# A decode kernel's projection and GLU: products over 32 equal columns, and zero products between them

## The chip, the core and the metric

The kernel runs on one core of a Trainium2 chip. The metric is the device time of one execution in microseconds (us), the median of several runs. Five engines work side by side and meet only at semaphores: TensorE (PE in the profile, its weight loads PEld) for matrix products into PSUM, VectorE (DVE), ScalarE (ACT), GpSimd (POOL) and SyncE (SP), whose queue here issues nearly all loads. 16 DMA engines carry the bytes.

## The reference

One token (D = 640) goes through a decoder layer: pre-norm attention over a cache of 4096 positions with 32 heads of 128, an output projection with a residual, then a pre-norm gated GLU with 1728 hidden columns and a second residual. Cut to what matters:

```python
def _A_ref(x, k_cache, v_cache, wq, wo):          # 32 heads, Dh = 128, Sk = 4096
    q = (x @ wq) per head
    scores = einsum("bhqd,bhkd->bhqk", q, k_cache) * Dh ** -0.5
    o = einsum("bhqk,bhkd->bhqd", softmax(scores), v_cache)
    return o.reshape(B, Sq, Hq * Dh) @ wo
def _B_ref(x, w_gate, w_up, w_down):
    return (gelu(x @ w_gate) * (x @ w_up)) @ w_down
h = x + _A_ref(_layernorm(x), k_cache, v_cache, wq, wo)
h2 = h + _B_ref(_layernorm(h), w_gate, w_up, w_down)
```

All inputs are bf16. The caches are 33.5 MB each, wq and wo 5.2 MB each, w_gate, w_up and w_down 2.2 MB each.

## The kernel before

**Order of the work.** Every engine has a list of operations written out by hand (class Prog). An operation waits for the semaphores of those that it depends on; products on TensorE run in the order of its list. `warm(e, n)` issues n products of a zero tile none_b with 512 columns into a PSUM bank that nobody reads then; `held` issues a product without a weight load of its own, so that the weights of the product before it are used again. In the profile, products that `held` issues have its line, L167.

**Start.** SP issues wq and the first K tile; ScalarE's queue issues x. GpSimd fills constants. TensorE runs 22 no-ops (L321), then x_cols (L325) turns x into columns, and a LayerNorm gives xlnB (L342; VectorE waits at L341 for the memset of xlnB first). q_proj (L354) waits for xlnB and wq.

**Attention.** Four tiles of 8 heads go through a loop on TensorE (L429). For each, VectorE multiplies K by q (L405), TensorE folds the products (L371), VectorE adds up the rest (L417), ScalarE takes the exponentials (L418), VectorE spreads them out (L424), and TensorE multiplies with V (L389) and sums by head (L395). Zero products stand in the loop in three places. K and V loads wait on SP until the tile that they overwrite has been read.

**Tail, which the change touches.** After the loop TensorE's list goes:
- z_sum (L464), the sums of the exponentials; VectorE then divides (L467, L468) and spreads out (L469), a product (L471) sorts, and VectorE copies to aP (L473).
- A product with the identity puts x into ps_p (L496).
- proj(0) and proj(16) (L501): 5 groups of outputs by 16 rows of wo each, 80 weight loads of 128 x 128 with one column of aP each. The first half waits for aP and the first half of wo, the second for the second half of wo. VectorE copies the result to hT (L507).
- LayerNorm (L331 to L337, with a product of the means at L332), hX (L515), and products that put the residual into ps_d (resid, L511), then hlnT (L518).
- glu (L531) twice, gate and then up: 75 weight loads with one column of hlnT each; the first waits for hlnT and w_gate, the second for w_up. VectorE and ScalarE make the GELU (L537 to L544) beside the second, and L545 multiplies with it.
- down (L552): 15 rows of products, four side by side in the array, then last_weights (L562) loads weights ahead, and the last four products (L565) wait for the last piece of w_down. VectorE and ScalarE copy (L567, L568), and two DMAs write the output.

SP's order in the tail: wo in two halves, small pieces of w_down into wd_lo, then, once the last V tile has been used, w_gate, w_up and four pieces of w_down (L491 to L493).

Of the kernel before, what the change touches and what calls it, by code (L numbers as in the profile page):

```python
# [7 lines left out]
ALU = mybir.AluOpType  # L8
# [156 lines left out]
def held(e, out, lhsT, rhs, start, stop):  # L165

    built = e.matmul(out, lhsT, rhs, start=start, stop=stop)  # L167
    old = built.ins
    bb = e.bass.cur_bb.bb
    new = mybir.InstMatmult(  # L170
        start_tensor_calc=old.start_tensor_calc, stop_tensor_calc=old.stop_tensor_calc, tile_size=old.tile_size,
        tile_position=old.tile_position, ldweights=False, name=old.name, engine=old.engine, debug=old.debug,
        ins=old.ins, outs=old.outs, sync_info=old.sync_info)
    insts = bb.instructions
    assert insts[-1].name == old.name
    del insts[-1]
    insts.append(new)
    return bass.BassInstruction(new)


def bass_sequential_preLN__gqa_block_cached__glu_gated_geglu__decode_kernel(nc, A_x, A_k_cache, A_v_cache, A_wq, A_wo, B_x, B_w_gate, B_w_up, B_w_down, out):
# [15 lines left out]
    xx = sb("xx", [128, 10], FP32)  # L197
    ln = sb("ln", [128, 8], FP32)
    xlnB = sb("xlnB", [128, 5, 64], BF16)
    hT = sb("hT", [128, 10], FP32)  # L200
    hX = sb("hX", [128, 128, 5], FP32)
    hlnT = sb("hlnT", [128, 5], BF16)
# [4 lines left out]
    aP = sb("aP", [128, 32], BF16)  # L207
    of_i = sb("of_i", [128, 32], BF16)
    g_t = sb("g_t", [128, 15], FP32)
# [3 lines left out]
    gu = sb("gu", [128, 15], FP32)  # L213
    hm = sb("hm", [128, 15], BF16)
# [4 lines left out]
    none_b = sb("none_b", [128, 128], BF16)  # L219
    wd_lo = sb("wd_lo", [64, 2, D], BF16)  # L220
    own_g = sb("own_g", [128, 15], FP32)
    id_f = sb("id_f", [128, 128], FP32)
# [7 lines left out]
    ps_g, ps_u, ps_p = bank[0], bank[1], bank[2]  # L230
# [4 lines left out]
    ps_z = bank[7]  # L235

    wo_sb = k_all[:, 0:32 * D].rearrange("p (i n) -> p i n", i=32)
# [3 lines left out]
    P = Prog(nc)  # L241
    V = lambda fn, *d: P.op("vector", fn, *d)
    A = lambda fn, *d: P.op("scalar", fn, *d)
    T = lambda fn, *d: P.op("tensor", fn, *d)
# [21 lines left out]
    def load_v(j, *after):  # L266
# [6 lines left out]
    c_xz = GP(lambda e: e.memset(xlnB[:, :, :], 0.0))  # L273
# [8 lines left out]
    c_idf = GP(lambda e: e.affine_select(id_f[:, :], ones_f[:, :], pattern=[[1, 128]], compare_op=ALU.is_equal,  # L282
                                         fill=0.0, base=0, channel_multiplier=-1), c_ones)
# [10 lines left out]
    for t in range(4):  # L294
        at = slice(32 * t, 32 * t + 32)
# [4 lines left out]
    for t in range(4):  # L300
        at = slice(32 * t, 32 * t + 32)
        c_of = GP(lambda e, at=at: e.affine_select(of_i[at, :], ones_b[at, 0:32], pattern=[[-1, 32]], compare_op=ALU.is_equal,
                                                   fill=0.0, base=0, channel_multiplier=1), c_of)
    c_none = GP(lambda e: e.memset(none_b[:, :], 0.0), c_of)
    GP(lambda e: e.memset(own_g[:, 0:13], 1.0))
    c_gm = GP(lambda e: e.memset(own_g[:, 13:15], 0.0), c_none)
    for lo in (0, 32):
        c_gm = GP(lambda e, lo=lo: e.affine_select(own_g[lo:lo + 32, 13:15], ones_f[lo:lo + 32, 0:2], pattern=[[0, 2]],
                                                   compare_op=ALU.is_ge, fill=0.0, base=15, channel_multiplier=-1), c_gm)
# [3 lines left out]
    def idle(eng, n):  # L313

        def fn(e):
            for _ in range(n):
                i = e.nop(hint="n", nofuse=True)
            return i
        return P.op(eng, fn)

    idle("tensor", 22)  # L321

    def x_cols(e):
        for c in range(5):
# [3 lines left out]
    xc = V(lambda e: e.tensor_copy(xx[:, 0:5], ps_s[:, 0:5]), xt)  # L328

    def layernorm(src, ev, out_fn, between=lambda: None):  # L330
        s2 = V(lambda e: e.tensor_mul(src[:, 5:10], src[:, 0:5], src[:, 0:5]), ev)  # L331
        m = T(lambda e: e.matmul(ps_s[:, 16:26], mean_f[:, :], src[:, 0:10], start=True, stop=True), s2, c_mean)  # L332
        l1 = V(lambda e: e.reduce_sum(ln[:, 0:2], ps_s[:, 16:26].rearrange("p (a c) -> p a c", a=2), axis=AX.X), m)
        l2 = V(lambda e: e.scalar_tensor_tensor(out=ln[:, 2:3], in0=ln[:, 0:1], scalar=ln[:, 0:1],
                                                in1=ln[:, 1:2], op0=ALU.mult, op1=ALU.subtract), l1)
        l3 = A(lambda e: e.activation(ln[:, 3:4], ln[:, 2:3], ACTF.Ln, bias=eps_t[:, 0:1], scale=-1.0), l2, c_eps)
        l4 = A(lambda e: e.activation(ln[:, 4:5], ln[:, 3:4], ACTF.Exp, bias=zero_t[:, 0:1], scale=-0.5), l3)  # L337
        between()
        return V(out_fn, l4)

    xz = P.op("vector", None, c_xz)  # L341
    xl = layernorm(xx, xc, lambda e: e.tensor_scalar(  # L342
        xlnB[:, :, :].rearrange("p c (a b) -> p c a b", a=4)[:, :, 0:4:3, :],
        xx[:, 0:5].unsqueeze(2).unsqueeze(3).to_broadcast([128, 5, 2, 16]), ln[:, 0:1], ln[:, 4:5],
# [27 lines left out]
            r = mm(e, bank[2 * i + s], id_b[:, :], prod[:, i, 32 * s:32 * s + 32, 16 * n:16 * n + 16], start=(n == 0), stop=(n == 7))  # L372
        return r

    def warm(e, n, load=False):
        for k in range(n):
            mm = e.matmul if load and k == 0 else lambda *a, **kw: held(e, *a, **kw)
            r = mm(ps_z, none_b[:, :], none_b[:, :].unsqueeze(1).to_broadcast([128, 4, 128]), start=True, stop=True)  # L378
        return r

    def fold(e, i):
# [40 lines left out]
    def block(j, s):  # L422
# [5 lines left out]
    T(None, c_idb, c_hs, c_none)  # L428
    lp = P.loop("tensor", range(NG), [  # L429
        ("wa", lambda e, j: warm(e, 8, True), lambda j: [landed["K", j, 0]], False),  # L430
        ("f00", lambda e, j: fold(e, 0), lambda j: [mults[j, 0, 0], reds[j - 1, 1] if j else qa], True),
        ("f01", lambda e, j: fold(e, 1), lambda j: [mults[j, 0, 1]], True),
        ("wb", lambda e, j: warm(e, 12), lambda j: [], False),
        ("f10", lambda e, j: fold(e, 0), lambda j: [mults[j, 1, 0], reds[j, 0]], True),
        ("f11", lambda e, j: fold(e, 1), lambda j: [mults[j, 1, 1]], True),
# [9 lines left out]
    for j in range(NG):  # L445
# [10 lines left out]
        if j < NG - 1:  # L456
# [2 lines left out]

    rt = GP(lambda e: e.tensor_tensor(out=RT[:, :, :], in0=RS[:, :].unsqueeze(2).to_broadcast([128, 2 * NG, 8]),  # L460
                                     in1=own8[:, :].unsqueeze(1).to_broadcast([128, 2 * NG, 8]), op=ALU.mult), exps[NG - 1, 1])
    def z_sum(e):
        for s in range(2):
            i = e.matmul(ps_z[:, 0:H], ones_f[:, :], RT[:, s::2, :], start=(s == 0), stop=(s == 1))  # L464
        return i
    z = T(z_sum, rt, c_ones)
    zr = V(lambda e: e.reciprocal(zt[:, :], ps_z[:, 0:H]), z)  # L467
    at = V(lambda e: e.tensor_tensor(out=aT[:, :], in0=ps_a[:, 0:H], in1=zt[:, :], op=ALU.mult), zr, lp.ev[NG - 1, "h"])  # L468
    as_ = V(lambda e: e.tensor_tensor(out=aS[:, :, :], in0=aT[:, :].unsqueeze(2).to_broadcast([128, H, 4]),  # L469
                                      in1=own[:, :].unsqueeze(1).to_broadcast([128, H, 4]), op=ALU.mult), at)  # L470
    sp = T(lambda e: e.matmul(ps_z[:, 32:64], aS[:, :, :].rearrange("p h q -> p (h q)"), of_i[:, :],  # L471
                              start=True, stop=True), as_, c_of)
# [20 lines left out]
    d_wd = [down_load(0, 0, 4), down_load(1, 0, 5), down_load(2, 0, 3), down_load(2, 3, 4)]  # L493


    T(lambda e: e.matmul(ps_p[:, 0:5], id_f[:, :], xx[:, 0:5], start=True, stop=False, skip_group_check=True), xc, c_idf)  # L496
    def proj(lo):
        def fn(e):
            for c in range(5):
                for i in range(lo, lo + 16):  # L500
                    r = e.matmul(ps_p[:, c:c + 1], wo_sb[:, i, c::5], aP[:, i:i + 1], start=False, stop=(i == 31),  # L501
                                 skip_group_check=True)
            return r
        return fn
    T(proj(0), ap, d_wo[0])
    pr = T(proj(16), d_wo[1])
    h = V(lambda e: e.tensor_copy(hT[:, 0:5], ps_p[:, 0:5]), pr)  # L507
    col = (0, 320, 160, 480)
    def resid(e):
        for q in range(4):  # L510
# [3 lines left out]
    def residual():  # L514
        hx = V(lambda e: e.tensor_tensor(out=hX[:, :, :], in0=id_f[:, :].unsqueeze(2).to_broadcast([128, 128, 5]),  # L515
                                         in1=hT[:, 0:5].unsqueeze(1).to_broadcast([128, 128, 5]), op=ALU.mult), h)
        T(resid, hx)
    hl = layernorm(hT, h, lambda e: e.tensor_scalar(  # L518
        hlnT[:, :], hT[:, 0:5], ln[:, 0:1], ln[:, 4:5], ALU.subtract, ALU.mult), residual)


    def glu(ps, w, cs, *deps):
        def fn(e):
            for c in cs:
                for m in range(15):
                    if m < 13:
                        lo, k = at_row[m]
                        ws = w[:, c, lo:lo + 127 * k + 1:k]
                    else:
                        ws = w[:, c, 16 * m - 208:16 * m - 80]  # L530
                    i = e.matmul(ps[:, m:m + 1], ws, hlnT[:, c:c + 1],  # L531
                                 start=(c == 0 and m == 0), stop=(c == 4), skip_group_check=True)
            return i
        return T(fn, *deps)
    ga = glu(ps_g, wg_sb, range(5), hl, d_wg)
    up = glu(ps_u, wu_sb, range(5), d_wu)
    g1 = V(lambda e: e.tensor_tensor(out=g_t[:, :], in0=ps_g[:, 0:15], in1=own_g[:, :], op=ALU.mult), ga, c_gm)  # L537
    g2 = V(lambda e: e.tensor_mul(t1[:, :], g_t[:, :], g_t[:, :]), g1)
    g3 = V(lambda e: e.scalar_tensor_tensor(out=t2[:, :], in0=t1[:, :], scalar=1.0 / GELU_C1, in1=g_t[:, :],
                                            op0=ALU.add, op1=ALU.mult), g2)  # L540
# [1 line left out]
    g7 = V(lambda e: e.tensor_scalar(t2[:, :], e_t[:, :], 1.0, None, ALU.add), g5)  # L542
    g8 = V(lambda e: e.reciprocal(t1[:, :], t2[:, :]), g7)
    g6 = V(lambda e: e.tensor_mul(gu[:, :], g_t[:, :], t1[:, :]), g8)  # L544
    g9 = V(lambda e: e.tensor_mul(hm[:, :], gu[:, :], ps_u[:, 0:15]), g6, up)  # L545

    def down(ms, qs=range(4)):
        def fn(e):
# [11 lines left out]
    def last_weights(e):  # L560
        for q in range(4):
# [4 lines left out]
                                start=False, stop=True), d_wd[3]) for q in range(4)]  # L566
# [35 lines left out]
```

The softmax here doesn't subtract the row's maximum and nothing guards it: scores larger than these inputs give would overflow.

## Time and profile before

| what | value |
| --- | --- |
| median of 7 runs | 201.99 us (201.87 to 202.56) |
| the profiled execution | 202.13 us |
| its span, first to last instruction | 200.9 us |
| PE, PEld, DVE busy | 137.8, 29.4, 103.7 us |
| bytes, mean rate | 84.31 MB, 420 GB/s |
| mean granted TensorE clock | 0.846 |

The page gives each engine's busy time; products overlap in the array, so PE's busy time is not the time in which columns stream through. The granted clock (PEclk) is given in parts of full speed. A line of the timeline has the start, the length, the engine, the line, the operation, the tiles, the count, and in brackets the idle time ahead and what ended it; a line can hold a group. The view by stage sums the engines' busy time over a stretch of the span. The chain that ended last follows back from the last instruction what released each.

### The profile page before, as it was taken

The numbers are of one execution on the slowest core, as the hardware profiler recorded it, in microseconds if no ns is written. First come the engines' busy times: TensorE is split into PE (matmuls) and PEld (weight loads), VectorE is DVE, ScalarE is ACT, GpSimd is POOL, SyncE is SP. The second block draws the span as 40 slices with busy tenths as digits, with TensorE's granted clock in tenths as the row PEclk, the third lists the DMA queues.
The fourth block names the chain that finished last, engine by engine and source line by source line (L and its number), as shares of the span: only waits on it lengthen the run. The fifth ranks groups of instructions, "written<-read, shape, count | busy, mean of one in ns | idle before, by whom it ended". The sixth has DMA issues, their size and how long they took to land.

```text
span 200.9 us, 2115 instructions
## 1 busy us (share of the span) xinstructions
PE 137.8 (69%) x1118; PEld 29.4 (15%) x742; DVE 103.7 (52%) x58; ACT 9.4 (5%) x27; POOL 7.3 (4%) x32
## 2 busy tenths in 40 slices
PE   0108001899887628898972589889789889778675
PEld 0103000000001300000031000000320000367574
DVE  0200001969945029998420596994996985120320
ACT  2100000000000100000000000000010000000100
POOL 6500000000000000000000000000000000200000
PEclk9999855569999957999998558999999999995555
DMA  9999999999999999999999999799999998999992
GB/s 327 449 478 418 418 418 418 418 418 470 509 447 431 418 431 418 418 418 431 418 418 418 418 522 496 320 405 418 437 509 418 418 431 385 424 432 416 427 402 114
DMA packets 2699, 84.31 MB, mean 420 GB/s; under 512 B 323, under 2 KB 518, under 8 KB 902
## 3 DMA queue, kind: packets, MB, share of 16 engines
q1 hardware_dynamic: 2690, 84.23, 97.8%
q8 instruction: 4, 0.07, 0.1%
q14 instruction: 1, 0.01, 0.0%
q10 hardware_dynamic: 4, 0.00, 0.0%
HBM read 84.23 MB, written 0.00 MB: 419 GB/s over the span
## 4 chain that ended last, share of the span: by engine, by line
DMA 51%; DVE 28%; PE 19%; ACT 1%; issue 1%; SPq 0%; DVEq 0%
DMA k_all<-in_A_k_cache_dram 42%; DVE prod L405 22%; PE psum L167 11%; DMA v_all<-in_B_w_up_dram 9%; PE psum L389 4%; DVE sc L417 3%; PE psum L531 1%; DVE p_bd L424 1%; PE psum L371 1%; PE psum L552 1%; DVE sc L414 1%; DVE sc L415 1%; PE psum L395 1%; ACT pt L418 0%; SPq L59 0%
## 5 line engine op out<-in xcount | busy, mean ns | idle before, releaser
L405 DVE TENSOR_TENSOR prod<-k_all,qb 128x8192 bf16<-128x8192 bf16 x16 | 70.3, 4420 | 41.1 <-DMA k_all<-in_A_k_cache_dram 35.5
L167 PE MATMUL psum<-prod,id_b 128*128 128x512 bf16 x240 | 58.7, 401 | 0.0
L167 PE MATMUL psum<-none_b 128*128 128x512 bf16 x132 | 35.0, 420 | 0.0
L378 PE MATMUL psum<-none_b 128*128 128x512 bf16 x4 | 2.2, 550 | 25.3 <-DMA k_all<-in_A_k_cache_dram 25.3
L389 PE MATMUL psum<-v_all,p_bd 128*32 128x512 bf16 x256 | 14.5, 380 | 4.7 <-DVE p_bd L424 4.7
L417 DVE TENSOR_REDUCE sc<-psum 128x128 f32<-128x2048 f32 x6 | 13.7, 2286 | 5.2 <-PE psum L167 5.2
L371 PEld LDWEIGHTS psum<-prod,id_b 128*128 128x128 bf16 x16 | 1.6, 97 | 77.5 <-issue 43.5
L371 PE MATMUL psum<-prod,id_b 128*128 128x512 bf16 x16 | 6.6, 414 | 8.6 <-DVE prod L405 5.8
L389 PEld LDWEIGHTS psum<-v_all,p_bd 128*32 128x32 bf16 x256 | 6.4, 97 | 37.1 <-DVE p_bd L424 30.9
L424 DVE TENSOR_TENSOR p_bd<-pt,own 128x1024 bf16<-128x1024 bf16 x8 | 9.8, 1222 | 2.2 <-ACT pt L418 2.2
L418 ACT ACTIVATE pt<-sc,zero_t 128x128 bf16<-128x128 f32 x8 | 3.2, 401 | 140.2 <-DVE sc L417 120.4
L354 PE MATMUL psum<-v_all,xlnB 128*32 128x512 bf16 x40 | 4.5, 630 | 6.9 <-DMA v_all<-in_A_wq_dram 6.9
L501 PE MATMUL psum<-aP,k_all 128*128 128x1 bf16 x160 | 6.7, 178 | 1.0 <-DMA k_all<-in_A_wo_dram 0.9
L460 POOL TENSOR_TENSOR RT<-RS,own 128x64 f32<-128x64 f32 x1 | 1.3, 1324 | 162.3 <-ACT pt L418 162.3
L501 PEld LDWEIGHTS psum<-aP,k_all 128*128 128x128 bf16 x160 | 6.6, 131 | 1.2 <-DMA k_all<-in_A_wo_dram 1.0
L395 PE MATMUL psum<-hs,po_sb 128*128 128x8 f32 x32 | 4.2, 258 | 3.2 <-ACT po_sb L458 3.2
L531 PE MATMUL psum<-hlnT,v_all 128*128 128x1 bf16 x150 | 5.5, 173 | 1.2 <-DMA v_all<-in_B_w_up_dram 1.2
L363 DVE CAST qb<-psum 128x512 bf16<-128x512 f32 x1 | 0.7, 692 | 9.9 <-PE psum L354 9.9
L531 PEld LDWEIGHTS psum<-hlnT,v_all 128*128 128x128 bf16 x150 | 5.3, 120 | 1.8 <-DMA v_all<-in_B_w_up_dram 1.3
L414 DVE TENSOR_REDUCE sc<-psum 128x64 f32<-128x1024 f32 x2 | 2.4, 1224 | 5.2 <-PE psum L167 5.2
L325 PE MATMUL psum<-one_bf,x_row 1*128 1x1 bf16 x5 | 0.4, 177 | 6.9 <-DMA x_row<-in_A_x_dram 6.9
L395 PEld LDWEIGHTS psum<-hs,po_sb 128*128 128x128 f32 x32 | 3.9, 191 | 5.1 <-issue 5.1
(75 smaller groups left out, 33.4 us busy)
## 6 DMA issues: line engine op xcount, KB each, us to landing
k_all<-in_A_k_cache_dram SPq DMA_DIRECT2D x2, 4096.0 KB, 19.1
v_all<-in_A_wq_dram SPq DMA_DIRECT2D x1, 5120.0 KB, 15.2
k_all<-in_A_wo_dram SPq DMA_DIRECT2D x2, 2560.0 KB, 29.2
v_all<-in_B_w_gate_dram SPq DMA_DIRECT2D x1, 2160.0 KB, 13.1
v_all<-in_B_w_up_dram SPq DMA_DIRECT2D x1, 2160.0 KB, 17.9
k_all<-in_B_w_down_dram SPq DMA_DIRECT2D x1, 800.0 KB, 20.5
k_all<-in_B_w_down_dram SPq DMA_DIRECT2D x1, 640.0 KB, 19.0
k_all<-in_B_w_down_dram SPq DMA_DIRECT2D x1, 480.0 KB, 21.1
```

The lines of the kernel that those rows point to most:

```text
L167: built = e.matmul(out, lhsT, rhs, start=start, stop=stop)
L354: i = e.matmul(ps_q[32 * t:32 * t + 32, :], xlnB[:, c, 32 * a:32 * a + 32], wq_j[:, c, t, a, :, :], start=(c == 0 and a == 0), stop=(c == ...
L371: mm = held if n or not first else lambda e, *a, **k: e.matmul(*a, **k)
L389: i = e.matmul(ps_o[a:a + 32, :], p_bd[:, s, 4 * b:4 * b + 4, :].rearrange("p g j -> p (g j)"), vt[:, 4 * b:4 * b + 4, :], start=(s == 0 a ...
L395: i = e.matmul(ps_a[:, bass.ds(at, 8)], po_sb[:, 128 * r:128 * r + 128], hs[:, r, :], start=(r == 0), stop=(r == 3))
L405: mults[j, s, i] = VM(lambda e: e.tensor_tensor(out=prod[:, i, :, :], in0=kt[:, 64 * c:64 * c + 64, :], in1=qb[:, j, :].unsqueeze(1).to_br ...
L414: V(lambda e: e.reduce_sum(sc[:, 64:128], g16(0, 1024), axis=AX.X), folds[j, s, 1], free)
L417: reds[j, s] = VR(lambda e: e.reduce_sum(sc[:, :], g16(0, 2048), axis=AX.X), folds[j, s, 1], free)
L418: exps[j, s] = AS(lambda e: e.activation(pt[:, :], sc[:, :], ACTF.Exp, bias=zero_t[:, 0:1], scale=INV_SQRT_DH, accum_out=RS[:, 2 * j + s:2 ...
L424: blocks[j, s] = VB(lambda e: e.tensor_tensor(out=p_bd[:, hf, :, :], in0=pt[:, :].unsqueeze(2).to_broadcast([128, 128, 8]), in1=own8[:, :] ...
L501: r = e.matmul(ps_p[:, c:c + 1], wo_sb[:, i, c::5], aP[:, i:i + 1], start=False, stop=(i == 31), skip_group_check=True)
L531: i = e.matmul(ps[:, m:m + 1], ws, hlnT[:, c:c + 1], start=(c == 0 and m == 0), stop=(c == 4), skip_group_check=True)
```

## The change

The 22 no-ops become one. VectorE's own wait for the memset goes; TensorE's x_cols waits for a later memset of the same engine, and VectorE waits for x_cols. The projection and both GLU products read their one column 32 times, and write 32 equal columns, of which one is read. Twenty-six zero products, with one weight load in each of five groups, are put into ps_u, the bank of the second GLU product: 3 ahead of z_sum, 4 behind it, 8 between the halves of the projection, 5 ahead of the residual products and 6 between the GLU halves.

```diff
-    idle("tensor", 22)
+    idle("tensor", 1)
...
-    xz = P.op("vector", None, c_xz)
...
-    def warm(e, n, load=False):
+    def warm(e, n, load=False, at=ps_z):
...
-            r = mm(ps_z, none_b[:, :], none_b[:, :].unsqueeze(1).to_broadcast([128, 4, 128]), start=True, stop=True)
+            r = mm(at, none_b[:, :], none_b[:, :].unsqueeze(1).to_broadcast([128, 4, 128]), start=True, stop=True)
...
+    T(lambda e: warm(e, 3, True, ps_u), c_none)
     def z_sum(e):
...
     z = T(z_sum, rt, c_ones)
+    T(lambda e: warm(e, 4, True, ps_u))
...
-    T(lambda e: e.matmul(ps_p[:, 0:5], id_f[:, :], xx[:, 0:5], start=True, stop=False, skip_group_check=True), xc, c_idf)
+    T(lambda e: e.matmul(ps_p[:, 0:160:32], id_f[:, :], xx[:, 0:5], start=True, stop=False, skip_group_check=True), xc, c_idf)
...
-                    r = e.matmul(ps_p[:, c:c + 1], wo_sb[:, i, c::5], aP[:, i:i + 1], start=False, stop=(i == 31),
+                    r = e.matmul(ps_p[:, 32 * c:32 * c + 32], wo_sb[:, i, c::5], aP[:, i:i + 1].to_broadcast([128, 32]), start=False, stop=(i == 31),
...
     T(proj(0), ap, d_wo[0])
+    T(lambda e: warm(e, 8, True, ps_u))
     pr = T(proj(16), d_wo[1])
-    h = V(lambda e: e.tensor_copy(hT[:, 0:5], ps_p[:, 0:5]), pr)
+    h = V(lambda e: e.tensor_copy(hT[:, 0:5], ps_p[:, 0:160:32]), pr)
...
+        T(lambda e: warm(e, 5, True, ps_u))
         T(resid, hx)
...
-                    i = e.matmul(ps[:, m:m + 1], ws, hlnT[:, c:c + 1],
+                    i = e.matmul(ps[:, 32 * m:32 * m + 32], ws, hlnT[:, c:c + 1].to_broadcast([128, 32]),
...
     ga = glu(ps_g, wg_sb, range(5), hl, d_wg)
+    T(lambda e: warm(e, 6, True, ps_u))
     up = glu(ps_u, wu_sb, range(5), d_wu)
-    g1 = V(lambda e: e.tensor_tensor(out=g_t[:, :], in0=ps_g[:, 0:15], in1=own_g[:, :], op=ALU.mult), ga, c_gm)
+    g1 = V(lambda e: e.tensor_tensor(out=g_t[:, :], in0=ps_g[:, 0:480:32], in1=own_g[:, :], op=ALU.mult), ga, c_gm)
...
-    g9 = V(lambda e: e.tensor_mul(hm[:, :], gu[:, :], ps_u[:, 0:15]), g6, up)
+    g9 = V(lambda e: e.tensor_mul(hm[:, :], gu[:, :], ps_u[:, 0:480:32]), g6, up)
```

## The prediction

> **What bounds the kernel now.** I read the page's slices first. The DMA row is full from the first slice to the last but one, so the kernel streams its 84 MB, and only what is left after the last bytes can be saved. Next I read the chain that ended last, in order of time, and the timeline of the tail.
>
> The chain's last pieces:
>
> ```profile
> 175.83 17.91 DMA v_all<-in_B_w_up_dram
> 193.74 0.04 issue
> 193.78 2.76 PE psum L531 x75
> ...
> 196.64 0.18 DVE hm L545
> 196.82 0.04 issue
> 196.86 2.13 PE psum L552 x32
> ```
>
> The up weights land at 193.74; the second GLU product, the product hm and the down projection follow without a gap. The chain does not name the other thing that is due, the last down weights. Their four loads are issued between 176.3 and 177.7 (the group of in_B_w_down_dram); the last is this DMA issue:
>
> ```profile
> k_all<-in_B_w_down_dram SPq DMA_DIRECT2D x1, 160.0 KB, 21.0
> ```
>
> 177.7 + 21.0 = **198.7**: the last four products (L565) can't start sooner. They start at 198.86, since L562 before them starts at 198.79. TensorE is thus only 0.1 us behind the DMA, and even waited for it:
>
> ```profile
> 198.43 0.23 PEld L552 LDWEIGHTS psum<-k_all,hm 128*1 128x1 bf16 x12 [0.18 <-DMA k_all<-in_B_w_down_dram]
> ```
>
> So a faster TensorE gains at most about 0.1 us of start, plus what a faster clock takes off the last products (0.29 us each): **0.15 us, under 0.1%**. A later TensorE costs in full.
>
> The clock, in the view by stage (columns: stage, length, PE busy and count, ..., PEclk, DMA share, GB/s):
>
> ```profile
> 173.34:176.75 3.41, 2.62 (x45) 1.36 (x38) 0.00 (x0) 0.59 (x1) 0.00 (x0) 1.00 1.05 450
> 176.75:180.16 3.41, 2.33 (x36) 2.14 (x36) 1.03 (x4) 0.00 (x0) 0.00 (x0) 1.00 0.97 414
> 180.00:181.00 1.00, 1.00 (x29) 1.00 (x28) 0.00 (x0) 0.00 (x0) 0.00 (x0) 0.58 0.84 362
> 183.58:186.99 3.41, 3.28 (x80) 3.19 (x80) 0.10 (x1) 0.00 (x0) 0.00 (x0) 0.50 0.99 421
> ```
>
> A mean of 0.58 over 180 to 181 puts the fall from 1.00 to 0.50 at 180.16. The trace's other changes (23.14, 43.62, 77.76, 108.48, 122.14, worked out alike) stand apart by multiples of 3.41 us, so I lay a grid of 3.41 us and ask how much of each interval had columns streaming through the array. A product of 512 columns follows the last by 0.216 us at clock 1.00, so 32 columns take 0.0135 us, and one takes nearly nothing. By that count the interval before 180.16 was some 5% full although "PE busy" says 2.33 of 3.41, and the clock fell; 173.34 to 176.75 (products of L389 to about 175.1) was 52% full, and it held. At 0.50, intervals up to 69% full left it low, 88% brought it back.
>
> **What the products of one column cost.** Two lines of the timeline, one at each clock:
>
> ```profile
> 179.19 3.28 PEld L501 LDWEIGHTS psum<-aP,k_all 128*128 128x128 bf16 x80 [0.16 <-DVE aP L473]
> 183.49 3.28 PEld L501 LDWEIGHTS psum<-aP,k_all 128*128 128x128 bf16 x80 [1.03 <-DMA k_all<-in_A_wo_dram]
> ```
>
> The first began at clock 1.00, the second ran at 0.50, and both took 3.28 us: 0.040 us per weight load. The GLU's 75 take 2.68 us, 0.036 each. The loads set the pace, not the clock: a faster clock gains **nothing** in projection and GLU.
>
> **Products of 32 columns: 310, in place of one.** Are 0.0135 us (0.027 at 0.50) added, or hidden behind the next load (0.036 to 0.040)? (Reading one column 32 times should cost nothing of itself: the zero products read 128 columns four times, at the usual 0.216.) The nearest rows:
>
> ```profile
> 176.19 0.97 PEld L395 LDWEIGHTS psum<-hs,po_sb 128*128 128x128 f32 x8 [1.28 <-issue]
> ...
> 177.07 0.53 PEld L464 LDWEIGHTS psum<-RT,ones_f 128*128 128x128 f32 x4
> ```
>
> With 0.19 for a last load, the pace is (0.97 - 0.19)/7 = 0.111 for products of 8 columns and (0.53 - 0.19)/3 = 0.113 for 32, though one of 32 lasts 276 ns against 256. For bf16:
>
> ```profile
> 148.59 0.81 PE L167 MATMUL psum<-none_b 128*128 128x512 bf16 x3
> 149.02 0.10 PEld L371 LDWEIGHTS psum<-prod,id_b 128*128 128x128 bf16 x1 [1.44 <-issue]
> 149.23 0.38 PE L371 MATMUL psum<-prod,id_b 128*128 128x512 bf16 x1
> ```
>
> The load starts with the last zero product, and the next product follows in the usual 0.216. Loads hide behind running products on the same rows. I take 0; the other end is 310 x 0.0135 = +4.2 us.
>
> [...]
>
> **The fills, one after the other,** at 0.216 us per product (clock 1.00):
> - 3 before the z sum: it is ready at once (RT was written by 171.9), so 177.07 moves by 3 x 0.216 = +0.65. Nothing hides it but the projection's wait (below).
> - 4 behind the z sum: 0.86, in the 1.0 us in which PE waits for aS: hidden.
> - Projection's first half: issues from 179.84 to 183.06. 8 fills: 1.73, to 184.8. The second half began at 183.50 (0.95 of waiting for wo): now at 184.85, **+1.35**. h and LayerNorm move along.
> - LayerNorm: the mean product took 0.60 (at 0.50); the like L496, begun at 178.72 and ended at 179.12 at clock 1.00, took 0.40: -0.20, leaving +1.15. 5 fills run behind it (1.08, about 188.9 to 190.0), within the wait for hX, which ends at 189.11 + 1.15 = 190.26. The residual products held PE 0.64 (189.16 to 189.80) at 0.50, so about 0.32 now. GLU's first half starts at 190.62, **+0.83** (hlnT, 189.35 + 1.15 = 190.50, is ready).
> - First half issues until 193.3; 6 fills, 1.30, to 194.60. wu has been there since 193.74: the second half starts at 194.62, **+0.84**. The GELU instructions hide beside it, as before.
> - Down starts at 196.86 + 0.84 = 197.70. It took 2.0 to L565, 1.95 without the remaining DMA wait; its groups of four products of 160 columns follow at 0.133, which the clock halves (its loads of one column overlap): about 1.25. L565 starts at **198.95**, against 198.86, past the 198.7 of the weights.
> - The last products 0.06 shorter. Sum: +0.09 - 0.06 = +0.03; with 0.02 for the longer last product of either half, **+0.05 us**.
>
> **What costs nothing.** 21 no-ops and VectorE's wait: x_cols starts when x lands (6.89), and the chain to xlnB ends at 9.91, 5.4 us before the wq products at 15.32; that cover would have to go first. Reading PSUM 32 columns apart: VectorE's instructions cost 0.17 for 5 and for 15 elements; I take 0, at worst twice that in the two on the path, +0.34. Instruction fetches (queue q8, four packets) will fall elsewhere in a stream with 31 instructions added and 21 taken out; no PE wait of the tail points to one now, 0 to +0.3. SP and POOL are not touched; DMA issues stay where they are.
>
> The profiled execution took 202.13 (span 200.9 and 1.2 around it), 0.14 over the median of 201.99. 202.13 + 0.05 - 0.14 = **202.04**, given as 202.05. About 0.2% (0.4 us) is what a measurement of this kernel can tell from no change.
>
> **Rivals.**
> - **The clock falls in the middle.** On the old grid the new intervals are full to: 53% (176.75: 7 fills, sums, start of projection), 43% (180.16: 2.9 us of projection at 0.0135/0.040 = 34%, two fills), 58%, 46%, 50%, 51%. The limit lies between 5% and 52%; another phase of the grid leaves some 38% in the barest. For: the limit may lie above. Against: most of the open stretch is below. Price: a fall at 183.58 makes 5.8 fills last twice as long, +1.25, and 203.3; a fall at the end makes down slow, +0.7, 202.7; a fall already at 180.16 makes all 8 fills slow, +1.7, 203.7. It decides once one interval is below the limit. **0.22**, slower.
> - **Loads don't hide the 32 columns.** +4.2, 206.2; decides if the pace exceeds 0.040. Against it are the two rows above. **0.08**, slower.
> - **TensorE is sooner than my sum, and the weights' landing decides.** -0.1 to -0.15: 201.85. A fill or LayerNorm 0.2 shorter suffices. **0.08**; 0.05 of it within 0.2%, 0.03 below by chance.
> - **The forecast**: **0.62**, 201.8 to 202.4; 0.57 within 0.2%, 0.03 slower by the unknown costs, 0.02 faster.
>
> Faster 0.03 + 0.02 = 0.05; slower 0.22 + 0.08 + 0.03 = 0.33; within 0.2% 0.62. The range goes from 201.75 to 203.6, taking in most falls of the clock, and leaves out the 206 and the worst falls.
>
> **What would show it.** PEclk 1.00 to the end; 80 loads in 3.3 us still; projection's second half at 184.85, GLU's halves at 190.6 and 194.6; L565 at 198.9 with no DMA wait before it. Wrong would be: a 0.50 after 180, a pace of 0.05 or more, or wd landing later than 198.7.

## The result and the profile after

The changed kernel took 204.08 us in the median of 26 runs (202.11 to 205.01), the kernel before 202.19 in 63 runs made beside it. The ratio is **1.0069** (95% interval 1.0051 to 1.0087): slower by 0.7%. The ratio agrees with the quotient of the means (203.77/202.37) and lies below that of the medians, because the 26 runs fall into three groups: 8 from 202.1 to 202.8, 5 from 203.4 to 203.8, and 13 from 204.4 to 205.0. The profiled execution took 203.62 us (span 202.4) against 202.13 (200.9): +1.49. It belongs to the middle group.

The chain that ended last, after, in order of time. Line numbers have moved: the zero products' loads are L377, proj L502, resid L513, glu L534, hm L549, down L556; the last four products are again under L167.

```profile
188.27 0.44 PE psum L377
188.71 1.71 PE psum L167 x4
190.42 0.64 PE psum L513 x8
191.06 2.68 PE psum L534 x75
193.74 0.23 PE psum L377
193.97 1.08 PE psum L167 x5
195.05 2.58 PE psum L534 x75
197.63 0.03 issue
197.66 0.02 DVEq L114
197.68 0.46 issue
198.14 0.18 DVE hm L549
```

The wait for the up weights has gone from the chain: zero products stand in its place, ahead of the residual products and ahead of the second GLU half. Between GLU and hm is a new 0.46 us of issue, where the chain of before had 0.04:

```profile
196.57 0.02 DVEq L114
196.59 0.04 issue
196.64 0.18 DVE hm L545
```

The view by stage for after (stage, length, busy time and count of PE, PEld, DVE, ACT and POOL, then PEclk, DMA share, GB/s):

```profile
177.68:181.09 3.41, 3.20 (x58) 2.37 (x55) 0.95 (x4) 0.00 (x0) 0.00 (x0) 1.00 0.93 400
184.51:187.92 3.41, 2.96 (x73) 2.86 (x71) 0.33 (x2) 0.00 (x0) 0.00 (x0) 1.00 0.97 416
187.92:191.33 3.41, 3.41 (x24) 0.73 (x21) 1.37 (x4) 0.59 (x2) 0.00 (x0) 0.50 1.00 423
194.75:198.16 3.41, 2.87 (x77) 2.66 (x75) 0.61 (x4) 0.00 (x0) 0.00 (x0) 1.00 0.70 274
198.00:199.00 1.00, 0.63 (x20) 0.38 (x24) 0.17 (x1) 0.00 (x0) 0.00 (x0) 0.58 0.05 15
```

The clock was at 0.50 for one interval from 187.92 and again from 198.16 (worked out from the mean of 0.58, as for before). Two lines of the timeline show what that does to the zero products:

```profile
182.48 1.67 PE L167 MATMUL psum<-none_b 128*128 128x512 bf16 x7
...
188.50 1.91 PE L167 MATMUL psum<-none_b 128*128 128x512 bf16 x4
```

Less the length of the last one (0.38 and 0.63, each product by itself), the first group follows at (1.67 - 0.38)/6 = 0.215 us, the second at (1.91 - 0.63)/3 = 0.427.

**Where the 1.49 us came from.** The last four products start at 200.35 instead of 198.86, so all of it arises ahead of them:

| step | before | after | later by |
| --- | --- | --- | --- |
| head sum (L395, now L394) starts | 176.19 | 175.48 | -0.71 |
| projection's second half | 183.50 | 183.99 | +0.49 |
| LayerNorm's sums (L333) | 187.95 | 188.31 | +0.36 |
| residual products | 189.16 | 190.35 | +1.19 |
| GLU's first half | 189.80 | 190.99 | +1.19 |
| GLU's second half | 193.78 | 194.88 | +1.10 |
| hm | 196.64 | 198.14 | +1.50 |
| last four products | 198.86 | 200.35 | +1.49 |

The five zero products at half clock add 0.83 (from +0.36 to +1.19), the gap ahead of hm 0.4. Down, which was to shrink from 2.0 to 1.25 us, ran at 0.50 and took as long as before (198.37 to 200.35). In this execution the tail began 0.71 earlier, which hides about as much of the fills' cost.

### The profile page after: what moved, and what is told of

It is laid out like the page before. It is cut to its first block, busy times and chain, and to the rows that moved or that the text cites. A ratio compares the mean times of both kernels' runs of the same rounds, so it can differ in the third digit from the quotient of the medians.

```text
span 202.4 us, 2124 instructions
## 1 busy us (share of the span) xinstructions
PE 141.0 (70%) x1144; PEld 30.1 (15%) x747; DVE 103.6 (51%) x58; ACT 9.4 (5%) x27; POOL 7.3 (4%) x32
## 4 chain that ended last, share of the span: by engine, by line
DMA 55%; DVE 23%; PE 19%; issue 1%; ACT 1%; SPq 0%; DVEq 0%
DMA k_all<-in_A_k_cache_dram 42%; DVE prod L404 19%; DMA v_all<-in_A_v_cache_dram 13%; PE psum L167 6%; PE psum L388 4%; PE psum L502 3%; PE psum L534 3%; DVE sc L416 1%; PE psum L556 1%; DVE p_bd L423 1%; DVE sc L413 1%; DVE sc L414 1%; PE psum L377 1%; PE psum L394 1%; PE psum L370 0%
## 5 line engine op out<-in xcount | busy, mean ns | idle before, releaser
L167 PE MATMUL psum<-prod,id_b 128*128 128x512 bf16 x240 | 56.0, 387 | 0.0
L167 PE MATMUL psum<-none_b 128*128 128x512 bf16 x153 | 41.2, 420 | 0.0
L377 PE MATMUL psum<-none_b 128*128 128x512 bf16 x9 | 4.3, 477 | 26.1 <-DMA k_all<-in_A_k_cache_dram 26.1
L370 PE MATMUL psum<-prod,id_b 128*128 128x512 bf16 x16 | 6.4, 401 | 9.4 <-DVE prod L404 6.6
L502 PEld LDWEIGHTS psum<-aP,k_all 128*128 128x128 bf16 x160 | 6.6, 131 | 1.7 <-DMA k_all<-in_A_wo_dram 1.4
L502 PE MATMUL psum<-aP,k_all 128*128 128x32 bf16 x160 | 6.7, 191 | 0.1
L394 PE MATMUL psum<-hs,po_sb 128*128 128x8 f32 x32 | 4.2, 258 | 3.2 <-ACT po_sb L457 3.2
L534 PEld LDWEIGHTS psum<-hlnT,v_all 128*128 128x128 bf16 x150 | 5.4, 119 | 1.6 <-issue 1.5
L534 PE MATMUL psum<-hlnT,v_all 128*128 128x32 bf16 x150 | 5.5, 186 | 0.0
L377 PEld LDWEIGHTS psum<-none_b 128*128 128x128 bf16 x9 | 1.4, 150 | 27.2 <-DMA k_all<-in_A_k_cache_dram 27.2
```

Source lines behind the costliest of these rows:

```text
L370: mm = held if n or not first else lambda e, *a, **k: e.matmul(*a, **k)
L377: r = mm(at, none_b[:, :], none_b[:, :].unsqueeze(1).to_broadcast([128, 4, 128]), start=True, stop=True)
L394: i = e.matmul(ps_a[:, bass.ds(at, 8)], po_sb[:, 128 * r:128 * r + 128], hs[:, r, :], start=(r == 0), stop=(r == 3))
L502: r = e.matmul(ps_p[:, 32 * c:32 * c + 32], wo_sb[:, i, c::5], aP[:, i:i + 1].to_broadcast([128, 32]), start=False, stop=(i == 31), skip_g ...
L534: i = e.matmul(ps[:, 32 * m:32 * m + 32], ws, hlnT[:, c:c + 1].to_broadcast([128, 32]), start=(c == 0 and m == 0), stop=(c == 4), skip_gro ...
```

## The experiments

All times stand against the kernel before, run beside each. Unless a part is named as left out, the computation is the reference's.

**e1: the 32 columns without the zero products** (all five `T(lambda e: warm(...))` of the change taken out).

> The changed kernel without its 26 zero products; the products over 32 columns, the one no-op and the missing VectorE wait stay. Theory A (the loss is the zero products' own time on the path, doubled where the clock has fallen; the 32 columns hide behind the weight loads): the tail goes back to that of before, projection's second half starts as wo lands, the second GLU half as wu lands, 80 loads still take 3.3 us; the time is that of before within 0.2% (0.1 us either way), whatever the clock does. Rival B (the 32 columns, or reading PSUM 32 columns apart, carry the loss): most of the +1.4 us stays. Rival C (the 0.46 us ahead of hm in the changed kernel, after the last GLU product had ended, comes of VectorE's list being one instruction shorter): that gap is seen here too, and +0.4 us stays.

Measured: **1.0002** (0.9985 to 1.0019), median 202.33. The timeline of e1:

```profile
179.14 3.28 PEld L500 LDWEIGHTS psum<-aP,k_all 128*128 128x128 bf16 x80 [0.16 <-DVE aP L472]
179.15 3.38 PE L500 MATMUL psum<-aP,k_all 128*128 128x32 bf16 x80
...
194.02 2.79 PE L530 MATMUL psum<-hlnT,v_all 128*128 128x32 bf16 x75 [1.16 <-DMA v_all<-in_B_w_up_dram]
```

80 loads take 3.28 us as before, and the second 80, at 183.73, 3.28 again, although the clock had fallen by then (the mean product behind them took 0.60 us, as at 0.50 before); the second GLU half waits for its weights again (and takes 2.79 us against 2.75 before). Products of 32 columns cost nothing here. The loss is not theirs: rival B falls. The gap ahead of hm, though, is here too: 0.53 between the last product's end (196.81) and hm (197.34).

**e2: the zero products without the 32 columns.**

```diff
-                    r = e.matmul(ps_p[:, 32 * c:32 * c + 32], wo_sb[:, i, c::5], aP[:, i:i + 1].to_broadcast([128, 32]), ...
+                    r = e.matmul(ps_p[:, 32 * c:32 * c + 1], wo_sb[:, i, c::5], aP[:, i:i + 1], ...
-                    i = e.matmul(ps[:, 32 * m:32 * m + 32], ws, hlnT[:, c:c + 1].to_broadcast([128, 32]),
+                    i = e.matmul(ps[:, 32 * m:32 * m + 1], ws, hlnT[:, c:c + 1],
```

> The changed kernel with products of one column again (written 32 columns apart, as the changed kernel reads them); all 26 zero products stay. Theory A, with a clock that falls once an interval of 3.41 us is less than some 35% full of streaming columns: the projection's halves and the GLU's no longer count, so the clock falls in more places and more of the zero products last 0.427 us instead of 0.216; slower than the changed kernel by 0.5 to 1.5 us, +2 to +3 against before. Rival B (the 32 columns are the loss): faster than the changed kernel by about 1 us. If the clock held without the 32 columns: the same as the changed kernel.

Measured: **1.0209** (1.0173 to 1.0244), median 206.60 of 5 runs: +4.4 us, more than expected. In its trace (timeline) the fills (zero products) ahead of both the second projection half and the second GLU half ran at half clock; less 0.63 for the last one they follow at 0.41 us, (3.06 - 0.63)/6, and at 0.43, (2.34 - 0.63)/4:

```profile
182.73 3.06 PE L167 MATMUL psum<-none_b 128*128 128x512 bf16 x7
...
195.72 2.34 PE L167 MATMUL psum<-none_b 128*128 128x512 bf16 x5
197.85 2.75 PE L534 MATMUL psum<-hlnT,v_all 128*128 128x1 bf16 x75
```

The second GLU half starts at 197.85, 4.1 us after before's. So the zero products are the cost, and the 32 columns make them cheaper: with them the loss is 0.7%, without them 2.1%.

**e3: fills sized by the waits of before** (0, 4, 3, 4, 4 in place of 3, 4, 8, 5, 6).

> The changed kernel with fewer zero products, sized by the waits of before: none ahead of the z sum, 4 behind it, 3 between the projection's halves (a wait of 0.95 us), 4 ahead of the residual products (1.3 us), 4 between the GLU's halves (1.2 us). Theory A: while the clock stays up no fill makes TensorE late; the second GLU half starts as wu lands and the end is set by the last down weights: 0.1 us below before; where the clock falls, up to +0.5. Median from -0.1 to +0.4 us against before. Rivals B and C: +0.5 to +1.4, as the 32 columns and the gap ahead of hm are still there.

Measured: **0.9989** (0.9969 to 1.0009), median 201.99. Its trace has the gap ahead of hm as well (hm at 197.39), and still the last four products started at 198.80, as down ran at full clock and took 1.2 us (48 products in 1.00 us, against 1.77 in the first trace of the changed kernel at 0.50):

```profile
197.85 1.00 PE L555 MATMUL psum<-k_all,hm 128*1 128x160 bf16 x48
198.80 0.23 PE L167 MATMUL psum<-k_all,hm 128*1 128x160 bf16 x4
```

Their weights had been issued at 177.8 with 21.0 us to landing: 198.8. In this execution the end is the landing. The change's loss is had back by taking 11 of 26 zero products out.

**e4: the start put back** (22 no-ops and VectorE's wait).

> The changed kernel with the 22 no-ops and VectorE's wait for the memset put back; everything in the tail stays. Theory A: the same as the changed kernel, +1.4 us (0.5 either way, as the clock's grid falls differently in each execution). Rival C (an instruction fewer on VectorE, or 21 no-ops fewer on TensorE, moved an instruction fetch to where it is waited for): the 0.46 us ahead of hm is gone from the trace, and the time is 0.4 us below the changed kernel.

Measured: **1.0043** (1.0011 to 1.0074), median 203.55. The chain of e4:

```profile
199.45 0.03 issue
199.48 0.02 DVEq L114
199.50 0.04 issue
199.54 0.18 DVE hm L550
```

0.04, not 0.46: the gap comes with the edit of the start, in a stage that had 5 us to spare. The time agrees in sign with rival C; the intervals of e4 and of the change overlap.

**e5: the kernel before without VectorE's wait**, and **e6: the changed kernel with the wait, but one no-op.** The edit, in opposite directions:

```diff
-    xz = P.op("vector", None, c_xz)
```

> The kernel before with one edit of the change alone: VectorE's own wait for the memset of xlnB is taken out. Rival C, now held as the second half of the theory (VectorE's list shorter by one makes the instruction after its last long wait come late): 0.46 us of issue ahead of hm in place of 0.04, the last four products 0.4 us later, +0.4 us (0.2%). If the gap came of the 32 columns, of reading PSUM 32 columns apart or of the fewer no-ops: no gap, and 0.0 us.

> The changed kernel with VectorE's wait put back alone; one no-op stays. Theory A with C: the gap ahead of hm is 0.04 again and 0.4 us of the changed kernel's loss go; about +0.9 us against before stay, which are the zero products' and the clock's. If the 21 no-ops had moved the fetch: the gap stays at 0.46, and the time at that of the changed kernel.

Measured: e5 **0.9998** (0.9980 to 1.0017), median 202.38 against 202.18; e6 **1.0032** (1.0008 to 1.0056), median 202.92. The timelines of e5, then of e6:

```profile
193.88 2.76 PE L530 MATMUL psum<-hlnT,v_all 128*128 128x1 bf16 x75 [1.24 <-DMA v_all<-in_B_w_up_dram]
...
197.17 0.17 DVE L544 TENSOR_TENSOR hm<-gu,psum 128x15 bf16<-128x15 f32 x1 [2.86 <-PE psum L530]
```

```profile
194.87 2.72 PE L535 MATMUL psum<-hlnT,v_all 128*128 128x32 bf16 x75
...
197.69 0.17 DVE L550 TENSOR_TENSOR hm<-gu,psum 128x15 bf16<-128x15 f32 x1 [2.30 <-PE psum L535]
```

The last product ends at 196.64 in e5 and hm starts 0.53 later; in e6 at 197.59, and 0.10 later. Over all 13 traces the gap is 0.52 or 0.53 in the seven without the wait and 0.10 or 0.11 in the six with it, whatever the no-ops, the columns and the fills. One instruction of VectorE, taken out at the start, makes hm 0.4 us late: that is shown. Why is not: a packet of the instruction queue q14 moves with it. The DMA view from 192.5 to 194.0 of before, and from 198.5 to 199.5 of after:

```profile
q14 instruction: 1, 0.01, 1.3%
```

```profile
q14 instruction: 1, 0.01, 3.0%
```

Before, the packet comes during the GELU, ahead of VectorE's long wait for the second GLU half; after, behind hm. In all six traces with the wait the packet lies 3.2 to 4.6 us ahead of hm, in all seven without it 0.7 to 0.9 us behind hm's start. So the packet moves with the edit; but one that comes after hm has begun is not what hm waited for, and what holds hm up stays open.

In time the price shows less clearly. e6 is 0.37% below the changed kernel (1.0069 - 1.0032; the intervals just overlap). In e5 the expected +0.4 us did not show in the ratio, and the median is +0.2. It shows at the lower end: none of e5's 13 runs is under 202.16, where 16 of the 35 of before are, and none of e1's 12 is under 202.26, where 16 of 29 are. The traced execution of e5 was its slowest (203.80); there the weights of down's last rows but one landed only at 200.1, after the whole delay.

**e7: e3 with the wait**, and **e8: the projection on 64 columns, with no fills between its halves.**

```diff
-                    r = e.matmul(ps_p[:, 32 * c:32 * c + 32], wo_sb[:, i, c::5], aP[:, i:i + 1].to_broadcast([128, 32]), ...
+                    r = e.matmul(ps_p[:, 64 * c:64 * c + 64], wo_sb[:, i, c::5], aP[:, i:i + 1].to_broadcast([128, 64]), ...
-    T(lambda e: warm(e, 8, True, ps_u))
```

> The fills of e3 (0, 4, 3, 4, 4) with VectorE's wait put back. Theory: TensorE is now up to 0.4 us ahead of e3 and waits for the last down weights, whose landing sets the end: 0.1 to 0.25 us below before, as e3 or 0.1 better, with fewer executions above it. It can't be 0.4 better than e3: the weights are not sooner. If TensorE and not the landing set the end of e3: 0.4 us below e3.

> As e7, with the projection on 64 columns and no fill between its halves (fills 0, 4, 0, 4, 4). At full clock 64 columns last 0.027 us and hide behind a load of 0.040, and they fill 67% of the time that loads take, above the 35 to 37% at which the clock falls in the runs so far. Theory: 80 loads still take 3.3 us; the clock stays at 1.00 through the first half; the wait of 0.9 us between the halves leaves intervals above 45%, so it holds until the LayerNorm at least; time as e7 within 0.2 us. If the load and the product share something (a rate below 1 per 0.040 us at 64 columns), 160 times the excess is added.

Measured: e7 **1.0002** (0.9986 to 1.0018), e8 **1.0002** (0.9989 to 1.0016). The timeline of e7's end:

```profile
196.83 0.30 PE L556 MATMUL psum<-wd_lo,hm 48*1 48x160 bf16 x8 [0.33 <-DVE hm L549]
197.06 0.79 PE L556 MATMUL psum<-k_all,hm 128*1 128x160 bf16 x36
198.45 0.38 PE L556 MATMUL psum<-k_all,hm 128*1 128x160 bf16 x12 [0.59 <-DMA k_all<-in_B_w_down_dram]
198.65 0.18 PE L566 MATMUL psum<-none_b,hm 128*1 128x1 bf16 x4
198.82 0.23 PE L167 MATMUL psum<-k_all,hm 128*1 128x160 bf16 x4
```

TensorE is 0.6 us ahead of before here and waits 0.59 us for the weights; nothing is gained: the last four products start at 198.82, against 198.86. In e8, the view by stage and a line of the timeline:

```profile
180.00:187.00 7.00, 5.75 (x140) 5.53 (x137) 0.28 (x2) 0.00 (x0) 0.00 (x0) 1.00 1.01 425
187.00:196.00 9.00, 7.17 (x147) 5.00 (x142) 2.54 (x11) 0.90 (x3) 0.00 (x0) 1.00 0.99 411
```

```profile
178.98 3.28 PEld L502 LDWEIGHTS psum<-aP,k_all 128*128 128x128 bf16 x80 [0.16 <-DVE aP L474]
```

64 columns hide behind a load of 0.040 us as well, and in this execution the clock held to 196.66 (worked out from a mean of 0.83 over 196 to 197), with 12 zero products instead of 26. That keeps the clock more cheaply, and the time is still that of before: none of e1, e3, e7 and e8 beats it beyond the interval.

**e9 and e10: the changed kernel again**, one execution each.

> The changed kernel unaltered, a second execution with a trace, to see its clock on another position of the 3.41 us grid. Theory: the time follows from the grid: where the intervals of the tail are all over some 37% full, the clock stays at 1.00 through the fills, the second GLU half starts at about 194.0, and the execution takes about 202.2 to 202.7; where one falls below, 203.4 to 205, and the trace shows fills of 0.427 us or down at half speed. Rival: the time varies with the landing of the weights, and the tail's clock is the same as in the first trace.

> The changed kernel unaltered, a third execution with a trace; theory and rival as for e9. Over the three traces, an execution slower by 1 us or more must show at least two more intervals at 0.50 in the tail.

Measured: 204.68 and 203.68. By the view by stage, e9's clock was at 0.50 from 182.80 to 186.21 and from 189.63 to 193.04, and full during down; e10's from 181.30 to 184.72 and from 198.37 on (worked out from means, as above). My expectation that a slower execution has more such intervals was wrong: both have two, like the first trace. What counts is what falls into them. The timelines of e9, then of e10:

```profile
182.90 3.19 PE L167 MATMUL psum<-none_b 128*128 128x512 bf16 x7
...
190.54 1.91 PE L167 MATMUL psum<-none_b 128*128 128x512 bf16 x4
```

```profile
182.74 2.65 PE L167 MATMUL psum<-none_b 128*128 128x512 bf16 x7
...
189.49 1.02 PE L167 MATMUL psum<-none_b 128*128 128x512 bf16 x4
```

In e9 nearly all of two groups ran slow, and the second GLU half began at 196.91; in e10 it began at 194.94. The weights w_up had landed by 193.9 in both, so this is not their landing. With 204.68, e9 stands for the largest group of the result's runs, the 13 from 204.4 up; the first trace and e10 stand for the middle one. In no trace of the changed kernel did the clock hold throughout. The eight executions from 202.1 to 202.8 have no trace; that the clock held where it mattered there is argued, not shown. Their mean granted clock does not tell: it is 0.897 in the run of 202.11 and in that of 203.63.

**e11: e7 without the last 160 KB of w_down.** One of the fifteen groups of the down projection's rows gets the weights of the group before it. The diff is cut to the load that goes; the last four products then read the rows before and wait for their load.

```diff
-    d_wd = [down_load(0, 0, 4), down_load(1, 0, 5), down_load(2, 0, 3), down_load(2, 3, 4)]
+    d_wd = [down_load(0, 0, 4), down_load(1, 0, 5), down_load(2, 0, 3)]
```

> e7 without the load of the last piece of w_down (160 KB); the last four products use the rows of the piece before it, so one of the fifteen groups of the down projection's rows gets other weights. Theory (the end is set by the last weights' landing, not by TensorE): the end comes sooner by the time of 160 KB at 420 GB/s, 0.39 us: 201.6 to 201.8, -0.1% to -0.3% against before. If TensorE's chain sets the end: as e7, 202.1.

Measured: **0.9981** (0.9968 to 0.9995), median 202.01 against 202.31; e7's ratio was 1.0002. The 0.2% agree with the 0.39 us expected for those bytes, and the traces agree with it: the last four products start at 198.46, against 198.82 in e7.

```profile
198.46 0.24 PE L167 MATMUL psum<-k_all,hm 128*1 128x160 bf16 x4
```

Fifteen zero products (e3, 198.80) or none (before, 198.86) left the start of the last four products where it was; 160 KB less moved it to 198.46. The intervals of e7 and e11 overlap, so this is support, not proof.

## Why the prediction was right or wrong, point by point

The forecast, 202.05 with the clock up to the end, did not come: its own sign of being wrong, a 0.50 after 180, is in all three traces. What came is the first rival, for which the range had been drawn up to 203.6. The ratio puts the change at 203.4 on the 201.99 of before, inside; the median of 204.08 is above.

- **The bound** (the last weights' landing leaves 0.15 us to gain): it held. TensorE 0.6 us ahead (e7) gained nothing; e3, the best, had -0.1% with an interval that takes in zero.
- **32 columns hide behind the loads**: right, in e1 and at 64 columns in e8. The other end of the estimate was 4.2 us more; e1 is 0.0% off, and its 80 loads take 3.28 us, as do those of e8.
- **The fills' own price**: right while the clock is full. The z sum came 0.65 later in relation to the head sum (1.56 us after it against 0.91), the four behind it cost nothing, the eight took 1.73 (182.26 to 183.99), as forecast.
- **The clock holds to the end**: this is the step that failed. I had left the limit between 5% and 52% full and put most of the chance on the side below my barest interval of 38%. Both were off. Counted the same way over all 13 traces, from each one's first fall on, the fullest intervals that were followed by a fall had 36% and, once, 38%, and the emptiest that held had 35% and 37%; that the count is good to two or three points is an estimate of mine. In these traces, then, the falls end and the holding begins at **35 to 38%**, right where I had put the design. Two intervals of the first trace show it: 177.68 to 181.09 has 0.59 us of zero products and 2.05 us of projection at 34%, 0.70, together 38%, and the clock held; 194.75 to 198.16 has 0.13 of a zero product and 75 x 0.0135 = 1.01, together 33%, and it fell. And the barest interval is barer than 38%: a stretch of 32-column products alone is 34% full (0.0135/0.040), and by my own times nothing but the projection's second half, 80 x 0.0135 = 1.08 us, lay between the fills that end at 184.8 and those that begin at 188.9, so an interval there is at most 32% full. In the trace, 184.51 to 187.92 holds 73 products, 29%, and the clock fell. It fell in every trace of the changed kernel, in different places, and twice in each; I had priced single falls, at 202.7 to 203.7. Where both fall on zero products (e9), it is 204.68.
- **The wait of VectorE costs nothing**: wrong. I looked for its cover at the start, where it was, and not at what the length of an engine's list does later. I had bounded fetches by +0.3, an estimate with no row behind it, on TensorE's stream, and taken 0; the gap is 0.4 and on VectorE.
- **Down takes 1.25 at full clock**: a little less where the clock was full (e9: 200.39 to 201.49 is 1.10), and 1.98 where it was not, as in the first trace.

The last four products start 200.35 - 198.95 = 1.40 later than the forecast had them. Step by step against the forecast: -0.71 for the early start of the tail (luck of this execution), +0.76 for the fills ahead of the residual products (190.35 against 189.59), +0.32 for those products at half clock, -0.10 for a GLU half that was a little shorter, +0.40 for the gap, +0.73 for down at half clock; that is 1.40. With the +0.03 of the forecast's own sum and the last products not shortened (0.06), 1.49.

## What to carry to other kernels

Ask first whether the path that a faster clock would shorten is limited by something that the clock drives: here 80 weight loads took 3.28 us at either clock, and the end waited for bytes (0.59 us in e7), so keeping the clock up could not pay for filler on the path. If the array has to be kept busy, widen products that hide behind their weight loads (64 columns in e8, with 80 loads in 3.28 us still), and size filler by the wait that it fills, at half clock (0.427 us a product here, against 0.215), as it runs at half clock just when the clock has fallen. An instruction that costs nothing where it stands may, as here, change what an engine does 190 us later: look at the first instruction behind the last long wait of every engine whose list has changed length.

## What the runs showed of the hardware

- In the trace of before the clock changed at 23.14, 43.62, 70.94, 77.76, 108.48, 122.14 and 180.16, between 1.00 and 0.50 (worked out from the means by stage): 6, 8, 2, 9, 4 and 17 times 3.41 us apart. Where the intervals lie differs from execution to execution (falls at 180.16 before, at 187.92, 182.80 and 181.30 in three executions of the changed kernel). By the count over the 13 traces, the fullest intervals after which the clock fell had 36%, and once 38%, of streaming columns, and the emptiest after which it held 35% and 37%, weight loads not counted (184.51 to 187.92 in the first trace has weight loads in 2.86 of its 3.41 us, and the clock fell). By the same count it came back after intervals of some 74 to 80%, and between 74 and 78% it also stayed low. In the trace of before it stayed at 0.50 after 111.90 to 115.31, with PE busy for 2.54 us, and came back after 118.72 to 122.14, with 3.42 us.
- A load of 128 x 128 bf16 weights took 0.040 us of the stream in the projection, where its columns lie five elements apart, and the same at either clock (80 of them 3.28 us at 179.04 in the changed kernel, at 1.00, and at 183.49 in the kernel before, at 0.50).
- One VectorE instruction fewer made an instruction 190 us later start some 0.42 us later after its wait had ended (0.52 or 0.53 us behind it in seven traces, 0.10 or 0.11 in six); the mechanism is open.
